# Seven-product sums seeded by a ScalarE copy in a second PSUM bank, and every engine's order given as a table

## The chip, the cores and the metric

The kernel runs on one core of a Trainium2 chip. The metric is the device time of one execution in microseconds, the median of several runs. The engines of the core are TensorE (PE in the profile; its weight loads are PEld), VectorE (DVE), ScalarE (ACT), GpSimd (POOL) and SyncE (SP). Here POOL issues the loads that cast from float32 to bfloat16, and some stores; SP issues transposing DMAs and the other stores.

## The reference

Sliding-window attention with a linear bias for 8 batches of 576 positions and 8 heads of 64, and then one mixer block on its output:

```
scores = q @ k.T / sqrt(64);  mask: 0 <= i - j < 128;  bias -slope[h] * |i - j|
x = softmax(scores) @ v                                  # (8, 576, 512)
h = relu(x.T @ w_tok1) @ w_tok2                          # 576 -> 256 -> 576, over positions
u = x + h.T
out = u + relu(u @ w_ch1) @ w_ch2                        # 512 -> 1536 -> 512, over channels
```

## The kernel before

The 576 positions of a batch are four blocks of 128 and a tail of 64; two batches share one tail block and make a pair (pairs 0 to 3). For each batch there is a *side* part (transposes of q and k, `scores`, exponentials, mask, `values`, then `token_mix`, which gives `u`) and a *main* part (the channel mixer). The side part of the next batch runs interleaved with the main part of this one. In the list of operations a plan's parts 2b+1 are main(b), and 2b are side(b).

The channel mixer's products are done as block products of a fast scheme with seven products instead of eight. `second` (L1246 and on) does so with `w_ch2`: each of the seven products is 128 x 256 outputs for two blocks, summed over six slices in two groups of six (`g` 0 and 1), L1326. They go to three banks: g2 takes products 1, 6, 7 and 4 one on top of the other, g1 product 2, g3 products 5 and 3. After product 1 a VectorE operation (`evict`, L1289) writes `ub` + g2 to an output tile `ob`; product 6 then adds onto g2, and when product 2 has ended in g1, a second `evict` adds g1 to that tile. The products stand in the order 1, 5, 6, 2, 3, 7, 4. `unit` (L976) does the same with `w_ch1` for some of the hidden slices (`UNITS`: nine units, in batches 3 to 7; the other slices go through `chunk`, L1085, as plain products): product 1 in bank y is copied to SBUF by `keep` (L1021, ScalarE), product 2 goes to bank z, and `join` adds the two on VectorE (L1030) and applies the ReLU (L1032). Product 6 adds onto y once the copy is made.

The banks: PSUM is eight banks of 128 x 512 float32. `plan.buf("ps", choice)` asks for one or for two side by side.

What sets the order. Nothing is issued as the code is read. Every step is an operation of a `Plan` with an engine, a cost, a rank and its dependences; `Plan.run` lets each engine take, greedily, the operation that is ready first (by the plan's costs), and among ready ones the lowest rank. Ranks are shifted by pseudo-random offsets (`SEEDS`, `SHIFT`). Some operations may go to ACT or to DVE, whichever would end first. The loads go on POOL's queue in the order of the list `LOADS` and then pair by pair; `qk` and `v` are rings of five blocks, so a load waits for the last user of the block that it overwrites. Where the plan sees PE idle in the first 60 us, `emit` puts products of zeros there (`spin`, L1418) that keep PE running.

The tail's way from token mix to channel mix: `token_mix` ends for the odd batch of a pair with products on half of the columns (L885), a VectorE sum writes `utl` (L907), a transposing DMA on SP makes `uTt` (L915), and `tail_piece` (L1129) multiplies it with `w_ch1`.

Of the kernel before, what the change touches and what calls it, by code (L numbers as in the profile page):

```python
# [10 lines left out]
ALU = mybir.AluOpType  # L11
# [8 lines left out]
class Buf:  # L20
    def __init__(self, ring, choice):
        self.ring, self.choice, self.slot = ring, choice, None
        self.writers, self.parts, self.users = [], {}, []
# [6 lines left out]
class Ring:  # L30
# [14 lines left out]
    def best(self, choice, skip=0):  # L45
        got = []
        for c in choice:
            ts = [self.free(i) for i in c]
            if None not in ts:
                got.append((max(ts), c))  # L50
        got.sort(key=lambda x: x[0])
        return got[skip] if len(got) > skip else None

    def take(self, b):
        b.slot = self.best(b.choice)[1]
        for i in b.slot:
            self.owner[i] = b
            self.log[i].append(b)
# [15 lines left out]
class Plan:  # L74
# [6 lines left out]
    def buf(self, name, choice=None):  # L81
        return Buf(self.rings[name], choice or self.rings[name].each)
# [46 lines left out]
    def run(self):  # L129
        ops = self.ops  # L130
        for o in ops:
            o.rank += SHIFT * offset(o)
# [82 lines left out]
        while todo:  # L215
            best = None
            for e, c in cand.items():
                pick, early = None, None
                for o in c:
                    if e == "POOL" and o is not pool[sent]:  # L220
                        continue
# [7 lines left out]
                    for b in o.bufs:  # L229
                        if b.slot is None:  # L230
                            got = b.ring.best(b.choice, asked.count(b.choice))
# [19 lines left out]
                if early and early[1] is not pick[1] and early[0][0] < pick[0][0] + GRACE * pick[1].cost:  # L251
# [13 lines left out]
            todo -= 1  # L265
            for b in o.bufs:
# [43 lines left out]
    def emit(self, spin):  # L310
        banks = self.rings["ps"]
        fills = []
        for a, z in self.gaps:
            if a < FILL and z - a > (250 if a > DENSE else 60):
                for i, log in enumerate(banks.log):
                    spans = [(min(u.t0 for u in b.users), max(u.done for u in b.users)) for b in log]
# [27 lines left out]
RELU = 350  # L344
SUMS_AT = 60e3
# [40 lines left out]
def kernel(  # L386
# [51 lines left out]
    def bank(choice=ONE):  # L438
        return plan.buf("ps", choice)
# [257 lines left out]
    def scores(pr, blk, half, rank, behind=()):  # L697
# [6 lines left out]
        sp = [bank(TWO + THIRD + [(6, 7)])] if joint else [bank(TWO + THIRD if first else TWO) for _ in range(2)]  # L704
# [13 lines left out]
        def go():  # L718
            for i in range(4):
                for kind, kb, a, z in work:  # L720
                    for e in range(2):
                        pe_.matmul(wide(e)[:, i, 0 if joint else kind, a:z],  # L722
                                   lhsT=ts[kb]()[e * D : (e + 1) * D, NHP + i, :],
                                   rhs=ts[blk]()[e * D : (e + 1) * D, i, a:z], start=not slanted, stop=True,
                                   skip_group_check=slanted)
# [105 lines left out]
    def token_mix(b, rank):  # L831
# [7 lines left out]
        t1 = [bank() for _ in range(NJ)]  # L839
# [20 lines left out]
        plan.op("PE", 225 if xt else 432, tails, rank(216), adds=t1,  # L860
# [11 lines left out]
        hts = []  # L872
        for blk in blocks:
            wide = b == 0
            if wide and blk < 2:
                hts.append(bank(TWO))
            ht = hts[blk % 2] if wide else bank()
# [3 lines left out]
            def go(blk=blk, ht=ht, hs=hs, fold=fold):  # L881
                for j in range(NJ):
# [4 lines left out]
                    else:  # L887
                        c = blk % NC
                        pe_.matmul(ht()[:, hs], lhsT=W2[:, j, c * P : (c + 1) * P], rhs=r1()[:, j, :],  # L889
                                   start=j == 0, stop=j == NJ - 1 and not fold)  # L890
# [5 lines left out]
            if blk == TAIL:  # L896
                rd += [(r1s[b - 1], j) for j in range(NJ)]
            tks = [(xb, (TAIL, 0)), (xb, (TAIL, 1))] if blk == TAIL and pr < HALVED else [(xb, (blk, None))]
            hop = plan.op("PE", 652 if fold else 436, go, rk, reads=rd + tks * fold, needs=lw2t if blk == TAIL else lw2,
                    mode=2 if blk == TAIL else 0, **({"adds": ht} if wide and blk > 1 else {"makes": ht}))  # L900
            if wide:
                wides.append(hop)
            if fold:
                plan.op("ACT", 600, lambda u=u_of(pr, blk)[1], ht=ht, hs=hs: act_.copy(out=u(), in_=ht()[:, hs]),
                        rk, part=u_of(pr, blk)[2], uses=[ht])
            else:
# [69 lines left out]
    def unit(b, u, rank, uT, tt, r2):  # L976

        y, z, w = [bank(ANY if b == B - 1 or BANKS == 8 else ONE) for _ in range(3)]
        e1, e2, e5 = [plan.buf("ob") for _ in range(3)]
# [56 lines left out]

        rk = product(1, y)
# [416 lines left out]
```

## Time and profile before

| | |
|---|---|
| three runs | 274.09, 274.43, 274.66 us; median 274.43 |
| profiled execution | span 273.4 us from its first to its last instruction, 1.0 less than the median of the runs |
| PE, PEld busy | 267.6 us (98%), 190.0 us (69%) |
| DVE, ACT, POOL busy | 230.4 us (84%), 148.9 us (54%), 112.9 us (41%) |
| granted TensorE clock | 0.999 |
| DMA | 38.71 MB, 142 GB/s in the mean |

In the rows of the profile a line stands with its engine, its operation and its tiles as out<-in. A busy PE includes the time in which a product waits in the array behind another, so its share says little by itself; the waits and the chain of work say more.

### The profile page before, as it was taken

How to read it: one execution, taken by the hardware profiler on the slowest of the kernel's cores; microseconds unless marked ns; L12 is line 12 of the kernel's file. 1: busy time of each engine (PE TensorE's matmuls, PEld its weight loads, DVE VectorE, ACT ScalarE, POOL GpSimd, SP SyncE). 2: the span in 40 equal slices, each digit the busy share in tenths (PEclk: the TensorE clock that was granted, in tenths of full speed). 3: DMA queues.
4: the chain of work that ended last, by engine and by line, in shares of the span. 5: the costliest groups of instructions: out<-in, count | busy, mean ns of one | idle time of the engine just before them, and what ended most of it. 6: DMA issues, size and time to landing. Idle time of an engine off the chain costs nothing.

```text
span 273.4 us, 7106 instructions
## 1 busy us (share of the span) xinstructions
PE 267.6 (98%) x2839; PEld 190.0 (69%) x2839; DVE 230.4 (84%) x543; ACT 148.9 (54%) x258; POOL 112.9 (41%) x142
## 2 busy tenths in 40 slices
PE   8999999999999999989999999999999999999994
PEld 4675667575568556765778868586578676888884
DVE  6577799998989499855999979998898899968984
ACT  5384895356931683038951079615960596047720
POOL 8999645950770077500890007800940300040000
PEclk9999999999999999999999999999999999999999
DMA  8999999999998999999999989999996800541016
GB/s 155 154 163 174 192 199 178 153 142 236 148 146 107 179 191 119 141 166 227 116 118 155 223 172 81 139 132 210 178 155 109 217 2 0 79 134 42 1 41 192
DMA packets 167553, 38.71 MB, mean 142 GB/s; under 512 B 155872, under 2 KB 166496, under 8 KB 167520
## 3 DMA queue, kind: packets, MB, share of 16 engines
q0 software_dynamic: 113936, 19.51, 91.7%
q1 hardware_dynamic: 51360, 18.10, 36.2%
q10 hardware_dynamic: 2224, 0.66, 1.2%
q8 instruction: 22, 0.36, 0.6%
q14 instruction: 11, 0.09, 0.1%
HBM read 35.85 MB, written 9.44 MB: 166 GB/s over the span
## 4 chain that ended last, share of the span: by engine, by line
PE 94%; DMA 3%; DVE 1%; issue 0%; DVEq 0%
PE ps L1326 25%; PE ps L1085 19%; PE ps L1006 10%; PE ps L802 7%; PE ps L722 7%; PE ps L847 5%; PE ps L889 4%; PE ps L1418 4%; PE ps L1129 4%; PE ps L1218 3%; DMA uTt<-utl 3%; PE ps L679 2%; PE ps L857 1%; PE ps L885 1%; PE ps L1070 1%; PE ps L924 1%
## 5 line engine op out<-in xcount | busy, mean ns | idle before, releaser
L535 POOL DMA_DIRECT2D v<-in_v_dram x40 | 34.5, 867 | 85.8 <-PE ps L802 84.0
L757 ACT ACTIVATE pe<-ps 128x1024 bf16<-128x1024 f32 (+1 forms) x62 | 56.0, 956 | 19.7 <-PE ps L722 19.5
L1085 PE MATMUL ps<-uT,WC 128*128 128x512 bf16 x232 | 55.4, 380 | 0.0
L1326 PEld LDWEIGHTS <-r 128*128 128x128 bf16 x372 | 35.8, 98 | 6.3 <-issue 0.8
L1091 ACT ACTIVATE r<-ps 128x512 bf16<-128x512 f32 x51 | 29.9, 599 | 18.4 <-PE ps L1085 18.1
L1085 PEld LDWEIGHTS <-WC 128*128 128x128 bf16 x232 | 21.1, 97 | 20.8
L535 POOL DMA_DIRECT2D qk<-in_q_dram x38 | 33.0, 878 | 2.8 <-DMA v<-in_v_dram 2.6
L535 POOL DMA_DIRECT2D qk<-in_k_dram x38 | 33.3, 890 | 1.4 <-DMA WC<-in_moe_w_ch_dram 1.0
L767 DVE TENSOR_TENSOR pe<-pe,mask 128x1024 bf16<-128x1024 bf16 (+1 forms) x50 | 32.4, 664 | 0.9 <-ACT pe L757 0.8
L1326 PEld LDWEIGHTS <-s 128*128 128x128 bf16 x288 | 27.6, 98 | 4.8 <-issue 0.5
L818 DVE TENSOR_TENSOR xb<-ps,rt 128x256 bf16<-128x256 f32 (+1 forms) x68 | 27.3, 416 | 0.7
L802 PEld LDWEIGHTS <-pe 128*128 128x128 bf16 (+1 forms) x560 | 22.4, 98 | 6.1 <-DVE pe L767 1.2
L802 PE MATMUL ps<-v,pe 128*128 128x65 bf16 (+1 forms) x560 | 26.1, 194 | 0.0
L1326 PE MATMUL ps<-WC,r 128*128 128x256 bf16 x192 | 24.4, 273 | 0.0
L1326 PE MATMUL ps<-WT,s 128*128 128x256 bf16 x192 | 23.9, 273 | 0.0
L1326 PE MATMUL ps<-WT,r 128*128 128x256 bf16 x180 | 22.1, 273 | 0.0
L722 PEld LDWEIGHTS <-qkT 64*128 64x128 bf16 x560 | 14.8, 94 | 10.5 <-issue 8.5
L744 ACT ACTIVATE pe<-ps 128x1024 bf16<-128x1024 f32 x7 | 7.2, 1022 | 26.1 <-PE ps L722 26.1
L907 DVE TENSOR_TENSOR ub<-ps,xb 128x512 bf16<-128x512 f32 x30 | 19.0, 683 | 0.8 <-PE ps L889 0.8
L722 PE MATMUL ps<-qkT 64*128 64x128 bf16 (+1 forms) x304 | 19.3, 216 | 0.1
L815 DVE RECIPROCAL rt<-ps 128x4 f32<-128x4 f32 (+1 forms) x76 | 12.6, 176 | 6.0 <-PE ps L802 5.1
L847 PE MATMUL ps<-xb,W 128*128 128x512 bf16 x64 | 16.4, 379 | 0.0
(118 smaller groups left out, 459.4 us busy)
## 6 DMA issues: line engine op xcount, KB each, us to landing
v<-in_v_dram POOLq DMA_DIRECT2D x32, 128.0 KB, 5.3
qk<-in_k_dram POOLq DMA_DIRECT2D x30, 128.0 KB, 5.4
qk<-in_q_dram POOLq DMA_DIRECT2D x30, 128.0 KB, 5.3
WC<-in_moe_w_ch_dram POOLq DMA_DIRECT2D x8, 384.0 KB, 10.0
out_dram<-raw SPq DMA_DIRECT2D x10, 256.0 KB, 2.5
out_dram<-raw SPq DMA_DIRECT2D x18, 128.0 KB, 3.1
out_dram<-ob SPq DMA_DIRECT2D x7, 256.0 KB, 2.5
out_dram<-raw POOLq DMA_DIRECT2D x5, 256.0 KB, 2.6
```

Source lines behind the costliest of these rows:

```text
L535: nc.gpsimd.dma_start(out=to()[p0 : p0 + n, :, :], in_=rows(src, b, s0, n))
L722: pe_.matmul(wide(e)[:, i, 0 if joint else kind, a:z], lhsT=ts[kb]()[e * D : (e + 1) * D, NHP + i, :], rhs=ts[blk]()[e * D : (e + 1) * D, ...
L757: act_.activation(out=pb()[:, e, :, lo:, c0:c1_], in_=wide(e)[:, :, lo:, c0:c1_], func=ACT.Exp, scale=scale)
L767: dve_.tensor_tensor(out=o, in0=o, in1=heads(mk, es), op=ALU.mult)
L802: pe_.matmul(view()[a:z, at, i, :], lhsT=pb()[:, e, i, kind, a:z], rhs=vb()[:, h, 0 : D + 1], start=m == 0, stop=m == len(mms) - 1, skip_g ...
L818: dve_.tensor_tensor(out=x4(), in0=view()[r0:r1_, :, :, 0:D], in1=rt()[r0:r1_, 0:n, :, :].broadcast_to([r1_ - r0, n, 4, D]), op=ALU.mult)
L847: pe_.matmul(t1[j]()[:, :], lhsT=W1[:, c, j * P : (j + 1) * P], rhs=xb()[:, blk, :], start=c == 0, stop=False)
L907: plan.op("DVE", 690, lambda blk=blk, u=u_of(pr, blk)[1], ht=ht, hs=hs: dve_.tensor_tensor(out=u(), in0=ht()[:, hs], in1=xb()[:, blk, :], ...
L1006: pe_.matmul(bk()[:, c * HS : (c + 1) * HS], lhsT=l(c, cb), rhs=r(cb), start=new and c == 0 and cb == 0, stop=cb == 1, skip_group_check=True)
L1085: pe_.matmul(ct()[:, :], lhsT=WC1[:, cb, t * P : (t + 1) * P], rhs=uT()[:, cb, :], start=cb == 0, stop=cb == NCB - 1)
L1091: plan.op("ACT", 600, lambda t=t, ct=ct: act_.activation(out=r2()[:, t, :], in_=ct()[:, :], func=ACT.Relu), rk, part=(r2, t), uses=[ct], o ...
L1326: pe_.matmul(of(bk, c), lhsT=l(t, c), rhs=w(t), start=first, stop=g == 1 and t == HK - 1, skip_group_check=True)
```

## The change

Three things change. First, where a later product's operand is the plain sum of two products, the first of the two is copied by ScalarE from its bank to a second bank, and the second product adds onto the copy there (a product that doesn't start a sum adds to what the bank holds). In `second` this takes the place of the `evict` after product 1 in batches 0 to 6: g2 is copied to g1, product 2 adds onto g1, and one `evict` brings both to the output tile. In `unit` it takes the place of the `keep` of product 1 and of a `join`: y is copied to z, product 2 adds onto z, and one ReLU (ScalarE, or VectorE where the table says so) reads z. A copy may also come ahead of the token mix's last products (`SEEDED`), but that list is empty.

Second, so that a product adds to the copy everywhere in the bank, the bank's last tenant must have been written by PE over its whole width. Such tenants are marked `full`; a bank for a copy (`seeded`) is only taken from one of them. The scores and the tail pieces start a sum once per bank, and not once per piece of it. No spin is put in a bank just ahead of a copy.

Third, `ORDER` lists for each engine its operations by number; `run` takes them in that order, and an operation that could go to ACT or DVE goes where the table has it. `SEEDS` has no effect on the order any more. POOL's loads are in the table too.

```diff
 class Ring:
-    def best(self, choice, skip=0):
+    def best(self, choice, skip=0, seeded=False):
         got = []
         for c in choice:
+            if seeded and not all(self.owner[i] is not None and self.owner[i].full for i in c):
+                continue
...
     def run(self):
         ops = self.ops
+        lists = {e: [ops[int(x)] for x in ORDER[e].split()] for e in ORDER}
+        for e, given in lists.items():
+            for o in given:
+                if o.eng != e:
+                    o.eng, o.cost, o.emit = o.other
+                o.other = None
+        at = dict.fromkeys(lists, 0)
...
-                    if e == "POOL" and o is not pool[sent]:
+                    if lists and o is not lists[e][at[e]] or not lists and e == "POOL" and o is not pool[sent]:
                         continue
...
+ORDER = {
+    "PE": """
+        162 161 159 157 192 179 163 194 166 169 168 170 176 173 181 186 189 205 199 207 212 202 215 224 221 218 225
...
+SEEDING = 600
+SEEDED = []
...
     def scores(pr, blk, half, rank, behind=()):
...
+                    new = not at and (not i if joint else i % 2 == 0) or not whole
                     for e in range(2):
                         pe_.matmul(wide(e)[:, i, 0 if joint else kind, a:z],
                                    lhsT=ts[kb]()[e * D : (e + 1) * D, NHP + i, :],
-                                   rhs=ts[blk]()[e * D : (e + 1) * D, i, a:z], start=not slanted, stop=True,
-                                   skip_group_check=slanted)
+                                   rhs=ts[blk]()[e * D : (e + 1) * D, i, a:z], start=new and not slanted, stop=True,
+                                   skip_group_check=True)
...
     def unit(b, u, rank, uT, tt, r2):
-        y, z, w = [bank(ANY if b == B - 1 or BANKS == 8 else ONE) for _ in range(3)]
-        e1, e2, e5 = [plan.buf("ob") for _ in range(3)]
+        y, z, w = [bank(ANY if b == B - 1 or BANKS == 8 else ONE, full=True, seeded=x == 1) for x in range(3)]
+        e2, e5 = [plan.buf("ob") for _ in range(2)]
...
         rk = product(1, y)
-        k1 = keep(e1, y, rk)
+        k1 = plan.op("ACT", SEEDING, lambda: act_.copy(out=z()[:, :], in_=y()[:, :]), rk, makes=z, uses=[y])
         rk = product(5, w)
         k5 = keep(e5, w, rk)
-        rk = product(2, z)
-        join(e1, z, up, lo, rk)
+        rk = product(2, z, [k1], False)
+        relu(z, up, lo, rk)
         rk = product(6, y, [k1], False)
...
     def second(b, rank, r2, ss, sums, ub):
-            evict(m, bk, *DONE[m])
+            if m == 1 and g1.seeded:
+                capt[1] = plan.op("ACT", SEEDING, lambda: act_.copy(out=g1()[:, :], in_=g2()[:, :]), rank(0) - EV,
+                                  makes=g1, uses=[g2])
+            else:
+                evict(m, bk, *DONE[m])
```

The next rows are in the order of the program, without times. First POOL's queue at the start, up to the first weights of the token mix (W_118 is W1, W1p its last 64 rows; qk and v are the blocks of the rings). Before, from the second load on:

```order
L535 DMA qk_68<-in_k_dram 64x8x64 x2
L535 DMA qk_67<-in_q_dram 128x8x64
L535 DMA qk_69<-in_k_dram 128x8x64
L535 DMA qk_69<-in_q_dram 128x8x64
L535 DMA v_72<-in_v_dram 128x8x64
L535 DMA v_73<-in_v_dram 128x8x64
L535 DMA v_74<-in_v_dram 128x8x64
L535 DMA v_75<-in_v_dram 64x8x64 x2
L535 DMA qk_68<-in_q_dram 64x8x64 x2
L535 DMA v_76<-in_v_dram 128x8x64
L535 DMA qk_70<-in_q_dram 128x8x64
L539 DMA W_118<-in_moe_w_tok_dram 128x4x256
```

and after, from the third on:

```order
L623 DMA v_72<-in_v_dram 64x8x64
L623 DMA qk_68<-in_k_dram 64x8x64
L623 DMA qk_69<-in_q_dram 128x8x64
L623 DMA qk_69<-in_k_dram 128x8x64
L623 DMA v_73<-in_v_dram 128x8x64
L623 DMA v_74<-in_v_dram 128x8x64
L623 DMA qk_68<-in_q_dram 64x8x64 x2
L623 DMA qk_68<-in_k_dram 64x8x64
L627 DMA W1p<-in_moe_w_tok_dram 64x256
L623 DMA v_75<-in_v_dram 128x8x64
L623 DMA v_76<-in_v_dram 128x8x64
L627 DMA W_118<-in_moe_w_tok_dram 128x4x256
```

Ahead of W1 stand, with the loads not shown (one whole block before, two after), nine whole blocks and six halves before, and eight wholes, five halves and W1p after.

Second, ScalarE in the main part of batch 5, where one unit and then the second products are done (pe is an exponential, r a ReLU, COPY to raw or ob the copy of a product to SBUF). Before:

```order
L1091 ACTIVATE r_103<-ps 128x512 x2
L757 ACTIVATE pe_87<-ps 128x1024 x2
L1091 ACTIVATE r_103<-ps 128x512 x2
L757 ACTIVATE pe_85<-ps 128x1024 x2
L824 ACTIVATE xb_92<-ps,rt_90 128x64 x4
L1021 COPY raw_107<-ps 128x512
L1021 COPY raw_108<-ps 128x512
L1021 COPY ob_110<-ps 128x512
L865 ACTIVATE r_98<-ps 128x512
L1034 ACTIVATE r_103<-r_103 128x2x256 x2
L1050 ACTIVATE r_103<-ps 128x2x256
```

and after:

```order
L848 ACTIVATE pe_85<-ps 128x1024 x2
L1194 ACTIVATE r_103<-ps 128x512
L1144 COPY ps<-ps 128x512
L848 ACTIVATE pe_86<-ps 128x1024
L1121 COPY ob_111<-ps 128x512
L1138 ACTIVATE r_103<-ps 128x2x256
L848 ACTIVATE pe_86<-ps 128x1024
L915 ACTIVATE xb_92<-ps,rt_91 128x64 x4
L1453 COPY ps<-ps 128x512
L956 ACTIVATE r_98<-ps 128x512
L1138 ACTIVATE r_103<-ps 128x2x256
```

The first of three copies to SBUF has become a copy from bank to bank (L1144), the unit lies between the exponentials now, and the copy of the second products (L1453) is new on this engine.

Third, SP's queue around the tail's transpose of pair 1 (the second pair, `uTt<-utl`). Before:

```order
L1303 DMA out_dram<-ob_110 128x256 x2
L668 DMA_TRANSPOSE qkT_80<-qk_67 128x8x128
L1306 DMA out_dram<-ob_111 128x2x256
L1306 DMA out_dram<-raw_108 128x2x256
L668 DMA_TRANSPOSE qkT_79<-qk_69 128x8x128
L915 DMA_TRANSPOSE uTt_102<-utl_95 128x4x128
L915 DMA_TRANSPOSE uT_101<-ub_94 128x4x128 x4
```

and after:

```order
L756 DMA_TRANSPOSE qkT_83<-qk_67 128x8x128
L756 DMA_TRANSPOSE qkT_80<-qk_71 128x8x128
L756 DMA_TRANSPOSE qkT_79<-qk_69 128x8x128
L1408 DMA out_dram<-ob_110 128x256 x2
L1408 DMA out_dram<-raw_109 128x256 x2
L1015 DMA_TRANSPOSE uTt_102<-utl_95 128x4x128
L1015 DMA_TRANSPOSE uT_101<-ub_94 128x4x128 x4
```

The transpose still stands ahead of the four of the batch; two stores of earlier batches are now what stands right ahead of it.

More of the change, by code (lines that the diff above doesn't have):

```diff
@@ L703, in scores @@
         joint = LOJOINT and lo and not slanted
-        sp = [bank(TWO + THIRD + [(6, 7)])] if joint else [bank(TWO + THIRD if first else TWO) for _ in range(2)]
+        whole = not slanted and c1_ - c0 == P
+        sp = ([bank(TWO + THIRD + [(6, 7)], full=whole)] if joint
+              else [bank(TWO + THIRD if first else TWO, full=whole) for _ in range(2)])
         pb = plan.buf("pe")
@@ L838, in token_mix @@
         r1 = plan.buf(f"r1{half}")
-        t1 = [bank() for _ in range(NJ)]
+        t1 = [bank(full=True) for _ in range(NJ)]
         tk = half if pr < HALVED else None
@@ L905, in token_mix @@
                         rk, part=u_of(pr, blk)[2], uses=[ht])
+            elif seed:
+                plan.op("ACT", 600, lambda u=u_of(pr, blk)[1], ht=ht: act_.copy(out=u(), in_=ht()[:, :]),
+                        rk, part=u_of(pr, blk)[2], uses=[ht],
+                        other=("DVE", 690, lambda u=u_of(pr, blk)[1], ht=ht: dve_.tensor_copy(out=u(), in_=ht()[:, :])))
             else:
@@ L1049, in unit @@
         rk = product(4, y, [j3], False)
-        mark(plan.op("ACT", 600, lambda: act_.activation(out=r2()[:, dn, lo], in_=half_of(y), func=ACT.Relu), rk,
-                     uses=[y], part=(r2, ("relu", dn.start, 0)),
-                     other=("DVE", 690, lambda: dve_.tensor_scalar(
-                         out=r2()[:, dn, lo], in0=half_of(y), scalar1=0.0, scalar2=None, op0=ALU.max))), dn)
+        relu(y, dn, lo, rk)
         return rk
@@ L1080, in chunk @@
         def chunk(t):
-            ct = first[t] if t < len(first) else bank()
+            ct = first[t] if t < len(first) else bank(full=True)
             def go(t=t, ct=ct):
```

74 lines of the change are left out of this document (52 added, 22 removed), and 54 rows, old and new, of the table ORDER.

## The prediction

> **What bounds it now.** I read the page first: its parts on busy time and on the chain that ended last.
>
> ```profile
> span 273.4 us, 7106 instructions
> PE 267.6 (98%) x2839; PEld 190.0 (69%) x2839; DVE 230.4 (84%) x543; ACT 148.9 (54%) x258; POOL 112.9 (41%) x142
> PE 94%; DMA 3%; DVE 1%; issue 0%; DVEq 0%
> ```
>
> TensorE is the chain nearly from end to end; VectorE, from which the change takes work, is 1% of it. So the next view is the waits, cut to PE: who held it up.
>
> ```profile
> PE ps L1418 <- DVE zero L499: 1.0, 1, 1.0
> PE ps L1129 <- DMA uTt<-utl: 0.9, 1, 0.9
> PE ps L924 <- DVE ub L907: 0.3, 1, 0.3
> ```
>
> Three waits, 2.2 us in all, one of them the first microsecond of the span. Not one is a wait for a copy, for a sum or for a bank in the seven-product parts. That doesn't mean that PE always did useful work: L1418 is `spin`, products of zeros that the planner puts where it expects PE to be idle. The windows and the chain, in order of time, show where:
>
> ```profile
> 0.00:20.00 20.00, 18.89 (x211) 12.11 (x212) 12.82 (x46) 11.71 (x19) 18.62 (x28) 1.00 1.80 158
> 140.00:160.00 20.00, 20.00 (x188) 16.36 (x186) 17.86 (x37) 4.26 (x7) 3.93 (x5) 1.00 1.52 180
> 220.00:240.00 20.00, 20.00 (x209) 15.18 (x205) 19.33 (x43) 10.77 (x20) 0.39 (x1) 1.00 0.20 29
> by line: PE ps L1418 33.0%; PE ps L679 11.8%; PE ps L722 10.0%; PE ps L802 8.6%; PE ps L1085 7.4%; PE ps L889 5.0%; PE ps L731 4.9%; PE ps L847 4.9%; PE ps L1070 2.4%; PE ps L924 1.8%; DVE ub L907 1.7%; PE ps L857 1.5%; DVE qkT L685 1.2%; P
> 1.00 3.27 PE ps L1418 x8
> 9.43 0.96 PE ps L1418 x5
> 20.57 0.84 PE ps L1418 x4
> 21.41 0.65 PE ps L847 x3
> ```
>
> The row "by line" is for the window 0 to 35 us: spins are 33.0% of it, 11.55 us, and they all lie before 30 us. From 40 us on PE has no hole that a view shows, but for the 0.9 us at L1129. In 220 to 240 us VectorE is at 19.33 of 20, so there it is close behind PE, but PE doesn't wait for it. What can be won is therefore in the start, in that one wait, and in the cost of PE's own changes between tilings; what can be lost is everywhere, since the order of every engine is new.
>
> **The parts, one by one.** Useful PE work stays the same. The two orders have 2839 and 2831 products; the eight that are gone are spins (51 before, 43 after).
>
> *Spins.* Counted in the two orders, the spins are 21,800 columns before and 18,624 after, 3,176 fewer. Priced by the mean of before, 11.55 us by 21,800 columns is 0.53 ns a column: −1.7 us. The two ends are the rows above: the first spin has 8 x 460 columns in 3.27 us (0.89 ns each, −2.8 us), the one at 9.43 has 5 of about 456 columns in 0.96 us (0.42 ns, −1.3 us). I take −1.7, the mean, since the spins that shrink are both early and late ones. This holds only if the waits under them really got shorter. What speaks for it is the order of the loads on POOL's queue, where each load is issued only after the one before:
>
> ```profile
> 1.37 2.42 POOL L535 DMA_DIRECT2D qk<-in_k_dram  x3 [0.30 <-issue]
> 5.65 0.89 POOL L535 DMA_DIRECT2D qk<-in_q_dram  x1
> 14.01 0.83 POOL L539 DMA_DIRECT2D W<-in_moe_w_tok_dram  x1
> 14.76 0.63 POOL L539 DMA_DIRECT2D W1p<-in_moe_w_tok_dram  x1
> 37.00 0.74 POOL L539 DMA_DIRECT2D WC<-in_moe_w_ch_dram  x1 [1.23 <-DMA WC<-in_moe_w_ch_dram]
> DMA to landing us min/median/max: 5.3/9.5/12.5
> 46.57 2.13 PE L1326 MATMUL ps<-WC,r 128*128 128x256 bf16 x18
> ```
>
> Ahead of W1 stood nine whole blocks and six halves; now it is eight wholes, five halves and the small W1p. A whole takes 0.89 us to issue, a half 0.77 (the x3 row is one whole and two halves), so 1.7 us less stand ahead, and W1p gives 0.6 of it back: W1 comes about 1.0 us earlier. PE's first use of W1 is the L847 row at 21.41, right behind a spin. The last piece of WC2, however, has the same loads ahead of it in both. It is issued at 37.00, and with the median of the weights' landings (9.5 us, the row of L539) it is there at 46.5; the second half of batch 0's first product needs it and is the second six of the eighteen from 46.57 on, at 47.2. That is a ceiling on what the start can win, and a rival below.
>
> A hole that no spin covers would cost more than its length. The first spin's 3,680 columns took 3.27 us, where 0.42 ns each gives 1.55: 1.7 us lost to a slow TensorE, while the clock in the window row already reads 1.00. The Trainium skill, "TensorE: Matmul & The Clock Gate", section "Part 1: The HAM clock gate", says that an idle window of about 3.4 us halves the clock until about as much busy time has passed; the start of this trace fits that, and its clock row doesn't show it. By that rule alone fewer spins are a risk: an estimate of 1.7 us for each uncovered hole of that length.
>
> *Changes of tiling on PE.* A row of sixteen score products (64 rows, run two at a time) and one of full products:
>
> ```profile
> 187.06 0.55 PE ps L722 x16
> 191.45 1.73 PE ps L1085 x8
> ```
>
> 1.73 by 8 is 0.216 us for 512 columns, so 0.054 for 128; sixteen in pairs are 0.43, and 0.12 remains for the change. In the two orders PE changes between whole, 64-row and half-wide tilings 99 and 94 times: 5 x 0.12 = −0.6 us; between 0 (if the changes that went were free) and −0.6.
>
> *Copies in place of sums.* In seven second products (all batches but the last) the sum after product 1 becomes a ScalarE copy from one bank to another; in nine units the copy to SBUF becomes a copy to a bank, and a sum and a ReLU become one ReLU.
>
> ```profile
> L1021 ACT COPY ob<-ps x8: 580/585/647, 137.1 to 252.3; 128x512 f32<-128x512 f32 x8
> L1289 DVE TENSOR_TENSOR raw<-ps,ub x20: 664/686/694, 51.2 to 264.7; 128x512 f32<-128x512 f32 x20
> L1030 DVE TENSOR_TENSOR r<-ps,raw x18: 661/684/692, 138.7 to 254.4; 128x512 bf16<-128x512 f32 x18
> L757 ACT ACTIVATE pe<-ps x62: 592/1018/1071, 7.9 to 223.9; 128x1024 bf16<-128x1024 f32 x52, 128x512 bf16<-128x512 f32 x10
> L1326 PE MATMUL ps<-WT,s 128*128 128x256 bf16 x192 | 23.9, 273 | 0.0
> ```
>
> VectorE loses 7 x 0.686 and 9 x 0.684, 11.0 us; part comes back, since the table gives it 11 more of the ReLUs of 512 columns and 7 of the tail's. None of it is on PE's path, so the term is 0, with 0.3 to win (the whole L924 wait). What could cost is the wait: product 2 and product 6 now both wait for the copy, and a copy that writes a bank is not in this trace. The nearest row is the copy to SBUF, 0.585. Shortest in the new order are three places (second products of batches 0, 2 and 4) where between the end of product 1 and product 6 lie 0.87 us of other PE work (four products of 512 columns, or their like). A product's end comes 0.165 us behind its slot (273 ns less 108 for 256 columns, half of 0.216), so the copy is done at 0.75: it holds by 0.1 us. From the other side: were ScalarE, which works in order, in the midst of an exponential of 1.02 us, the copy would be up to 0.9 us late, 16 copies 14 us. In the order the copies mostly stand behind exponentials whose scores ended 1.3 us or more earlier. I take 0.
>
> *The tail's transpose.* The one wait for a DMA, in order of time:
>
> ```profile
> 110.47 0.60 PE ps L885 x4
> 111.09 0.69 DVE utl L907
> 111.81 6.84 DMA uTt<-utl
> 118.69 1.03 PE ps L1129 x8
> 110.05 1.44 POOL L535 DMA_DIRECT2D qk<-in_q_dram  x2
> ```
>
> Before, 6.6 us of PE work stand between the product that makes `utl` (L885) and the first that uses it transposed (L1129); after, eleven groups of products with 5.5 us (six of 0.66, three of 0.43, two of 0.12). The transpose took 6.84 us because it was issued just behind a burst of loads (last row). With the same 6.84 us the wait would be 2.0 instead of 0.9 us, +1.1; in the new order the burst is released by values products that end about 4.6 us ahead of L885, not 4.3, and it is longer; if it has drained, −0.9. I take 0.
>
> **Sum.** −1.7 − 0.6 + 0 + 0 = −2.3, and 0.3 back for small late arrivals of a new order: −2.0. The profiled execution has a span of 273.4; the runs' median is 274.4, 1.0 more, and I keep that: 271.4 of span, **272.4 us**.
>
> **Rivals.**
> - *More is won.* The burst of loads has drained and the early spins were the ones that shrank: another 0.9 and 0.4, 271.1 us. Chance 0.15.
> - *The start is bound by the loads.* The second half of product 1 begins at 46.5 instead of 47.2, no earlier, and by the two orders 0.4 us more of other work stands ahead of it: 1.1 us won instead of 1.7; and the tail's wait grows by 0.5. Then −1.1 − 0.6 + 0.5 + 0.3 = −0.9, 273.5 us. For it speaks that POOL issues for 18.62 of the first 20 us. Chance 0.13.
> - *Slower: PE waits for the copies.* ScalarE's queue holds them behind exponentials and ReLUs that themselves wait for later products. From a mean of 0.125 us late over the 16 copies the gain of 2.0 is gone; with 0.2 us each, 3.2 us, it is 275.6. For it: three places hold by 0.1 us, and the bank copy has no row. Against it: no wait of PE for ACT in the trace, with copies just as close. Chance 0.22.
> - *A cold TensorE.* One hole in the start that the table doesn't foresee and no spin covers: the 1.7 us of the first spin lost once more, 274.1, no change. Chance 0.06.
> - *The change doesn't do what it says*, in that the copies would not spare VectorE: by the counts above it does, and VectorE isn't the bound. No chance of its own.
>
> The forecast has the remaining 0.44. 0.2% of the median, about what a measurement of this kernel can tell, is 0.55 us, so "the same" is 273.9 to 275.0. Faster: 0.44, 0.15 and most of the load-bound case, 0.69. Same: the cold case and the edge of two others, 0.08. Slower: 0.23. The range goes from 270.2 (both ends of the spins' price and the drained burst) to 275.6, the price of the late copies; it leaves some 0.05 below and 0.12 above.
>
> **What would show it.** Right: spins at about 9.8 us of the chain in the first 35 us instead of 11.55; L847 first at about 20 us; no wait of PE for ACT in the list of waits; the copies at about 0.59 us. Wrong: waits of PE for the ACT lines of the copies (L1144, L1453 of the new kernel), a wait at the tail's first product near 2 us, or holes after 40 us that stand in no term above.

## The result, and the profile after

The changed kernel runs in 278.06 us (median of four, 276.87 to 279.58), the kernel before, beside it on the same chip, in 274.26 (four, 273.83 to 274.66): a ratio of 1.014, interval 1.010 to 1.018. That is 3.8 us slower where 2.0 us faster was forecast, and outside the range.

First the page of the kernel after, its busy times and the engines of the chain that ended last:

```profile
span 276.3 us, 7051 instructions
PE 265.7 (96%) x2799; PEld 189.0 (68%) x2831; DVE 229.2 (83%) x542; ACT 145.4 (53%) x268; POOL 112.9 (41%) x142
PE 69%; DMA 12%; DVE 8%; issue 3%; ACT 3%; POOL 2%; SPq 1%; ACTq 0%; DVEq 0%
```

TensorE's share of the chain fell from 94% to 69%, and a quarter of the chain now runs through transfers, VectorE and ScalarE. (2831 products were loaded; 32 of their records are missing, so the busy time of PE says little. The loads are all there, and what follows goes by them.) Its list of waits, cut to PE, where before there were three:

```profile
PE ps L1232 <- DMA uTt<-utl: 1.1, 1, 1.1
PE ps L1528 <- DVE zero L587: 1.0, 1, 1.0
PE ps L767 <- DVE qk L638: 0.5, 2, 0.3
PE ps L813 <- DMA qkT<-qk: 0.5, 2, 0.3
PE ps L893 <- DVE r L1195: 0.4, 1, 0.4
PE ps L1188 <- DVE r L1195: 0.2, 1, 0.2
PE ps L813 <- DVE ob L1337: 0.2, 1, 0.2
PE ps L893 <- DVE pe L858: 0.2, 1, 0.2
```

The first two were there before (0.9 and 1.0). The rest is new and small: the casts of the raw blocks, head transposes, ReLUs, a sum, a mask. None is a wait for a copy. The copies themselves, from the groups:

```profile
L1144 ACT COPY ps<-ps 128x512 f32<-128x512 f32 x9 | 5.1, 582 | 13.0 <-PE ps L1106 12.9
L1453 ACT COPY ps<-ps 128x512 f32<-128x512 f32 x7 | 4.1, 580 | 7.5 <-PE ps L1432 7.4
```

They last 0.58 us (0.59 was expected), and between the end of each and the first product that needs it lie 0.05 to 2.28 us; ten of the sixteen have under 0.57.

To see where PE falls back, I weigh its products by their columns and ask when a given amount of useful work was done. What is left after that work is taken off is the time lost up to there (spins, waits, changes of tiling). The column "before, usual" is an execution of the same instructions in the same order (`buffer_before` below); the one whose profile the prediction shows has 1.2 us more from 104 us of work on, of which more later. Each column is one execution.

| useful work done, us | before, shown | before, usual | after | after with both mends and a buffer | redrawn from 17 us on |
|---|---|---|---|---|---|
| 16 | 15.27 | 15.10 | 14.69 | 14.87 | 15.14 |
| 24 | 16.11 | 15.93 | 15.97 | 16.16 | 16.04 |
| 32 | 16.26 | 16.08 | 16.63 | 16.81 | 16.34 |
| 96 | 19.84 | 19.66 | 20.10 | 20.36 | 19.48 |
| 104 | 21.23 | 20.08 | 21.70 | 20.87 | 19.69 |
| 144 | 22.49 | 21.35 | 23.73 | 22.76 | 21.16 |
| 224 | 24.80 | 23.65 | 26.74 | 25.06 | 23.65 |

After wins 0.4 to 0.6 us by 16, has lost it by 24 to 32 (40 to 49 us of the trace), and then loses, above all between 104 and 144 (125 to 168 us) and near 192. Against the usual execution of before it has also lost 1.2 us between 96 and 104, at the tail's transpose, where the shown one lost as much. The first loss is on VectorE. The window from 34.4 to 43.1 us of before, then of after, and pieces of after's chain in it:

```profile
34.40:43.10 8.70, 8.70 (x111) 5.20 (x109) 8.33 (x19) 7.76 (x15) 3.25 (x4) 1.00 1.50 195
```

```profile
34.40:43.10 8.70, 7.84 (x94) 4.74 (x94) 8.23 (x20) 7.17 (x10) 5.01 (x6) 1.00 1.41 198
```

```profile
34.43 0.18 DVE rt L906
...
36.46 1.29 DVE pe L858 x2
37.78 0.69 DVE r L1195
...
42.42 0.59 DVE r L1195
43.01 0.04 issue
43.06 1.02 PE ps L1188 x4
```

VectorE is as full as before (8.23 of 8.70), but now the chain stays on it from 34.4 to 43.1 us, and PE, which had no idle time there, is busy for 7.84. Twice a ReLU that frees a bank (37.78, 42.42) stands behind masks and normalisations.

The later loss has two roots. One is the order of SyncE. Of the 53 transposes, two landed less than 0.5 us ahead of their first product before; now seven do, five of them head transposes by 0.05 to 0.11 us. The worst of the loads that wait, and SyncE's queue ahead of it:

```profile
192.74 0.45 PEld L813 LDWEIGHTS <-qkT 64*128 64x128 bf16 x16 [0.78 <-DMA qkT<-qk]
185.08 5.43 SPq L756 DMA_TRANSPOSE qkT<-qk  x4
```

The transpose it waits for is the third of those four; its blocks had been in SBUF since 144.2 us, and the second, ahead of it, isn't needed before 195.6. (The load of head transposes at 189.13 us, which waits for no transfer, has 0.42 us of idle time ahead of it too, so about half of the 0.78 is the wait. PE's own row there books 0.3.)

The other is the buffers. Six hold a sum (or a kept product of a unit), a sum from the time VectorE begins it until its store has landed. This sum was complete at 91.5 us, and its store is issued at 217.8:

```profile
90.82 0.68 DVE L1394 TENSOR_TENSOR raw<-ps,ub 128x512 f32<-128x512 f32 x1
217.81 1.76 SPq L1408 DMA_DIRECT2D out_dram<-raw  x2
```

Over the 31 stores of whole sums that stand in SyncE's and GpSimd's lists, the time between the end of the sum and the issue of its store adds up to 550 us in after, 76 us in before (longest 7.7). With buffers parked like that, the others turn over so fast that VectorE meets a store that hasn't landed, and TensorE behind it waits for a bank (rows of VectorE and of PE):

```profile
158.00 0.69 DVE L1394 TENSOR_TENSOR ob<-ps,ub 128x512 f32<-128x512 f32 x1 [0.57 <-DMA out_dram<-ob]
159.41 0.21 PE L813 MATMUL ps<-qkT 64*128 64x128 bf16 x1 [0.18 <-DVE ob L1337]
```

Last, the end. Before, the tail's four stores were issued from 263.5 us on, and the last store landed 1.8 us after its issue. After, they are issued from 268.95 us on, three microseconds before PE's last product ends (before: six), and the last store takes 2.7 us:

```profile
268.95 2.40 SPq L1346 DMA_DIRECT2D out_dram<-raw  x4
271.44 1.09 SPq L1411 DMA_DIRECT2D out_dram<-ob  x2
272.63 0.44 SPq L1482 DMA_DIRECT2D out_dram<-raw  x1
```

### The profile page after: what moved, and what is told of

Read it like the earlier page. It is cut to its first block, busy times and chain, and to the rows that moved or that the text cites. A ratio compares the mean times of both kernels' runs of the same rounds, so it can differ in the third digit from the quotient of the medians.

```text
span 276.3 us, 7051 instructions
## 1 busy us (share of the span) xinstructions
PE 265.7 (96%) x2799; PEld 189.0 (68%) x2831; DVE 229.2 (83%) x542; ACT 145.4 (53%) x268; POOL 112.9 (41%) x142
## 4 chain that ended last, share of the span: by engine, by line
PE 69%; DMA 12%; DVE 8%; issue 3%; ACT 3%; POOL 2%; SPq 1%; ACTq 0%; DVEq 0%
PE ps L1432 18%; PE ps L1188 13%; PE ps L1106 9%; PE ps L813 6%; DMA qkT<-qk 5%; PE ps L893 5%; PE ps L938 4%; PE ps L981 4%; PE ps L1232 3%; PE ps L1322 2%; DMA raw<-in_k_dram 2%; DMA uTt<-utl 2%; DVE pe L858 2%; ACT pe L848 2%; DMA qk<-in_q_dram 1%
## 5 line engine op out<-in xcount | busy, mean ns | idle before, releaser
L848 ACT ACTIVATE pe<-ps 128x1024 bf16<-128x1024 f32 (+1 forms) x62 | 56.8, 958 | 40.5 <-PE ps L813 38.7
L1194 ACT ACTIVATE r<-ps 128x512 bf16<-128x512 f32 x40 | 22.9, 600 | 12.6 <-PE ps L1188 12.4
L893 PEld LDWEIGHTS <-pe 128*128 128x128 bf16 (+1 forms) x560 | 23.6, 98 | 7.3 <-DVE pe L858 1.4
L893 PE MATMUL ps<-v,pe 128*128 128x65 bf16 (+1 forms) x560 | 26.9, 194 | 0.9 <-DVE r L1195 0.4
L909 DVE TENSOR_TENSOR xb<-ps,rt 128x256 bf16<-128x256 f32 (+1 forms) x62 | 25.0, 415 | 0.8
L1432 PE MATMUL ps<-WC,r 128*128 128x256 bf16 x192 | 25.4, 273 | 0.0
L1432 PE MATMUL ps<-WT,s 128*128 128x256 bf16 x192 | 24.9, 273 | 0.0
L1007 DVE TENSOR_TENSOR ub<-ps,xb 128x512 bf16<-128x512 f32 x30 | 19.9, 682 | 1.9 <-PE ps L981 1.9
L1411 POOL DMA_DIRECT2D out_dram<-raw x5 | 3.6, 720 | 39.0 <-issue 27.8
L915 ACT ACTIVATE xb<-ps,rt 128x64 bf16<-128x64 f32 (+1 forms) x56 | 12.7, 338 | 7.2 <-DVE rt L906 7.2
```

What stands on the lines that cost most here:

```text
L848: act_.activation(out=pb()[:, e, :, lo:, c0:c1_], in_=wide(e)[:, :, lo:, c0:c1_], func=ACT.Exp, scale=scale)
L893: pe_.matmul(view()[a:z, at, i, :], lhsT=pb()[:, e, i, kind, a:z], rhs=vb()[:, h, 0 : D + 1], start=m == 0, stop=m == len(mms) - 1, skip_g ...
L909: dve_.tensor_tensor(out=x4(), in0=view()[r0:r1_, :, :, 0:D], in1=rt()[r0:r1_, 0:n, :, :].broadcast_to([r1_ - r0, n, 4, D]), op=ALU.mult)
L915: act_.activation(out=x4()[:, e, i, :], in_=view()[r0:r1_, e, i, 0:D], func=ACT.Copy, scale=rt()[r0:r1_, e, i, :])
L1007: plan.op("DVE", 690, lambda blk=blk, u=u_of(pr, blk)[1], ht=ht, hs=hs: dve_.tensor_tensor(out=u(), in0=ht()[:, hs], in1=xb()[:, blk, :], ...
L1194: plan.op("ACT", 600, lambda t=t, ct=ct: act_.activation(out=r2()[:, t, :], in_=ct()[:, :], func=ACT.Relu), rk, part=(r2, t), uses=[ct], o ...
```

## The experiments

All times are medians; "before" is the kernel before, beside them on the same chip (273.9 to 274.1 us). The numbers in the diffs are entries of the table, that is, operations.

**sp_mended.** Four entries of SyncE's list, pieces of it one to a line:

```diff
- 608 459 301 632 620
+ 608 632 459 301 620
- 868 948 869 870 595 463 867 964
+ 948 868 869 870 867 595 463 964
- 1092 1116 1104 1128
+ 1092 1104 1116 1128
```

> The changed kernel's table with four places of SyncE's list altered and nothing else: the head transpose issued at 90.89 us goes ahead of two stores, the one at 146.48 ahead of a u transpose, the u transpose at 151.51 ahead of two stores, and the one at 187.81 ahead of the one at 186.44. Three of them land 0.05 to 0.11 us before the first product that reads them in the changed kernel. Theory T (the table leaves no room, so TensorE waits for late transposes): the waits that the profile books at TensorE's loads for these tiles, 0.4 us near 151 us and 0.8 us near 192 us, shrink to the 0.3 of an ordinary switch of tiling, and the kernel ends 0.3 to 1.0 us earlier, about 277.4. Rival C (the time is lost to the copies in ScalarE): within 0.2 us of the changed kernel.

276.81 us, ratio 1.0109 (1.0092 to 1.0126). That is 1.25 less than the changed kernel, which ran on another chip; by the intervals of the two ratios a gain is likely, its size isn't settled. In its profile the wait near 192 us is gone, and the mend at 146 us cost something: two stores came later for it, and TensorE waited 0.7 us near 155 us for a sum that had no buffer.

**end_mended.** TensorE's, VectorE's and SyncE's lists:

```diff
- 1400 1413 1420 1416 1417 1414 1407 1427
+ 1400 1413 1407 1416 1417 1414 1420 1427
- 1360 1421 1418 1415 1384 1408 1401 1429
+ 1360 1401 1408 1418 1384 1415 1421 1429
- 1422 1409 1404 1430
+ 1404 1409 1422 1430
```

> The changed kernel's table with its last 15 us altered and nothing else: the last six products of the tail's second half trade places with a half product, so that the tail's last two sums and its four stores stand about 2 us earlier on VectorE and SyncE, and TensorE does as many products in as much time. Theory E (the tail's stores are still under way when the last stores are issued): the last store lands 1.8 us after its issue, as before the change, in place of 2.7, the span is 0.8 to 1.0 us shorter, and the 1.7 us outside the span may fall back to 1.0; 276.3 to 277.3. Rival: the landing is long for another reason; within 0.3 us of the changed kernel. If the sums now come late for the product that waits for them, TensorE loses 0.2 to 0.4 us there.

276.18, ratio 1.0083 (1.0066 to 1.0100). The tail's stores are issued at 266.26 instead of 268.95; the last store is issued at 272.45 (on ScalarE's queue, so it isn't among these rows of SyncE's), as late as in the changed kernel (272.63), and lands 1.75 us later, at 274.2 instead of 275.3:

```profile
266.26 2.41 SPq L1346 DMA_DIRECT2D out_dram<-raw  x4
269.09 0.40 SPq L1411 DMA_DIRECT2D out_dram<-raw  x1
270.01 1.72 SPq L1411 DMA_DIRECT2D out_dram<-ob  x2
271.83 0.41 SPq L1482 DMA_DIRECT2D out_dram<-raw  x1
```

So theory E holds, for 1.1 us of landing in these two profiles. PE's last product ends no earlier (271.9 against 272.0 us), since this execution has a wait of its own in the middle, for a u transpose in an order that wasn't touched there:

```profile
PE ps L1188 <- DMA uT<-ub: 1.1, 1, 1.1
```

The time outside the span did not fall: it is 1.7 to 1.8 us in every timed execution of both kernels.

**sp_end_mended.** Both.

> Both mends of the table together. If they do not touch each other the gains add: theories T and E 275.8 to 276.9, still above the kernel before; rival C: no change.

275.82, ratio 1.0068 (1.0055 to 1.0081): clearly better than the change, and still 1.9 us behind before. Its profile has a new largest wait, the one that the later stores brought:

```profile
155.25 0.42 DVE L1337 TENSOR_TENSOR ob<-ps,utl 128x256 f32<-128x256 f32 x1 [1.32 <-DMA out_dram<-ob]
155.73 0.81 PE L1322 MATMUL ps<-WT,r 128*128 128x256 bf16 x6 [0.97 <-DVE ob L1337]
```

**sums_in_table.** The old sums in the new order; the two edits in the unit, `seeded` taken from the bank of the second product (its sum then stands in VectorE's list), and every PSUM tile pinned to the bank that it has in the changed kernel. The kept product of a unit takes one of the six buffers again, as before the change:

```diff
-        k1 = plan.op("ACT", SEEDING, lambda: act_.copy(out=z()[:, :], in_=y()[:, :]), rk, makes=z, uses=[y])
+        k1 = keep(e1, y, rk)
...
-        rk = product(2, z, [k1], False)
-        relu(z, up, lo, rk)
+        rk = product(2, z)
+        join(e1, z, up, lo, rk)
```

> The old sums put back in the new order: the first products of the seven-product sums are kept and added by VectorE and ScalarE as before the change, each new addition standing on VectorE where the copy stood on ScalarE (or just ahead of the relu), everything else in the table's order and in the same PSUM banks. Rival C (the copies cost the time): faster than the changed kernel, 274 to 277. Theory T (the copies are covered, the order is what loses): slower than the changed kernel, since the additions queue behind other work of VectorE in an order that was drawn without them; 16 places with 0.05 to 2.3 us of room behind the copy, so 2 to 8 us, 280 to 286.

287.22, ratio 1.0483 (1.0469 to 1.0497): 9 us slower than the change, a little more than expected. VectorE works 238.3 us instead of 229.2, and PE now waits for what it and ScalarE keep and join:

```profile
PE ps L1137 <- ACT ob L1152: 2.0, 1, 2.0
...
PE ps L924 <- DVE r L1161: 1.3, 2, 0.9
```

Rival C, that the copies cost the time, falls. In this order they spare it; that says nothing yet on whether they gain in another.

**copies_twice.** Each copy done twice, in both places:

```diff
-lambda: act_.copy(out=z()[:, :], in_=y()[:, :])
+lambda: [act_.copy(out=z()[:, :], in_=y()[:, :]) for _ in range(2)]
```

> The changed kernel with each of its 16 copies into the second bank done twice, so that it is through about 0.57 us later; nothing else differs. The room between the end of a copy and the first product that adds up on it or overwrites what it read is 0.05 to 2.3 us in the changed kernel's profile; 10 of the 16 have under 0.57, and what they lack adds up to 2.3 us. Theory T (TensorE does not wait for the copies as they are, and the cover is thin): 1.5 to 2.5 us slower than the changed kernel, 279.5 to 280.6. Rival C (TensorE waits for copies already): 16 times 0.57, 9 us slower. If the cover is wide: no change.

281.57, ratio 1.0270 (1.0254 to 1.0286), 3.5 us slower than the change. The two rows of waits for the copies add up to 2.1 us, what the room lacked (2.3):

```profile
PE ps L1106 <- ACT ps L1144: 1.2, 3, 0.5
...
PE ps L1432 <- ACT ps L1453: 0.9, 3, 0.3
```

Another 1.4 us came behind them (0.8 of it booked to a u transpose that landed late). So the copies are covered as they are, and the cover is thin, as theory T had it; what a delay sets off further on was left out of the expectation.

**copies_by_the_rules.** `ORDER = {}`: the copies without the table.

> The copies alone: the table is left out, and the planner's rules draw the order as before the change, with the numbers that shift ranks as they were. Theory T: those numbers were fitted to the old sums, and a product that is copied must now stand ahead of the one that adds up on it; slower than both kernels, 280 to 300. Rival (the copies gain by themselves and the table spoils it): 271 to 274.

296.12 (two executions), ratio 1.0798 (1.0778 to 1.0818), inside what theory T expected. The copies need an order drawn for them; the rules' numbers, as they are, give a bad one.

**redrawn_with_room.** 204 of TensorE's 514 places, 305 of VectorE's 509, 96 of GpSimd's 137, 61 of SyncE's 82 and 53 of ScalarE's 201 differ from the changed kernel's table.

> The change whole, with its copies; the table is drawn once more, by moving single entries of the five lists and keeping what shortens the plan when every transpose and load is taken to land 0.4 us (or transposes 0.7 us) later, every operation of VectorE and ScalarE to last 12 ns longer and every wait to be answered 20 ns later than the kernel's planner assumes. The end is as in the mended kernel. Theory T (the table loses because nothing in it may come late): the waits that the mended kernel still shows on TensorE behind 30 us (1.0 us for a sum that stood behind a store, 0.4 and 0.3 for relus, 0.3 to 0.5 for head transposes) go, and 2 to 3.5 us with them: 272.3 to 273.8, no slower than the kernel before. Rival (the copies and the new reach of the PSUM banks cost something that no order gives back): 275 or more.

278.07, ratio 1.0129 (1.0108 to 1.0149). That is 4 us above the range of theory T, and as a time it is what the rival foresaw; the profile shows another reason than the rival's. The late transposes are gone from its waits. In their place VectorE's timeline has a copy that waits for a store, and PE's list of waits a product that waits for what VectorE does behind that copy:

```profile
166.17 0.69 DVE L1122 COPY raw<-ps 128x512 f32<-128x512 f32 x1 [2.33 <-DMA out_dram<-raw]
```

```profile
PE ps L1106 <- DVE xb L909: 2.2, 1, 2.2
```

Stores had not been among the things taken to be late. This miss led to the buffers.

**one_more_buffer.** Both mends, and

```diff
-    plan.ring("ob", raws + [sb.tile([P, DM], F32, name=f"ob{i}") for i in range(2)])
+    plan.ring("ob", raws + [sb.tile([P, DM], F32, name=f"ob{i}") for i in range(3)])
```

> The table with both mends, and a seventh buffer for the sums that are stored, in place of six. In the mended kernel VectorE waits 1.3 us at 155 us for a store to land before it may write into its buffer, and TensorE waits 1.0 us behind it. Theory T (small waits of this kind are the rest of the loss): 0.5 to 1.0 us faster than the mended kernel, 274.8 to 275.3. Rival: the buffer was not the limit, within 0.2.

274.49, ratio 1.0020 (1.0009 to 1.0032): 1.3 us better than the same without it, and 0.4 us slower than before. VectorE's wait for a store is 0.6 us in its profile instead of 1.3, and PE's wait behind it 0.2 instead of 1.0.

**one_store_earlier.** One entry:

```diff
- 301 632 620 789
+ 301 632 451 620 789
- 1251 1263 451 1317
+ 1251 1263 1317
```

> One entry of SyncE's list moved and nothing else: the store of a sum that VectorE finishes at 91.5 us, and that the changed kernel issues at 217.8 us, is issued at about 92. Theory S (six buffers hold the sums until they are stored; the table leaves one full for 126 us, so the others turn over too fast for their stores to land): VectorE's wait for a store near 158 us (0.57 us) goes, with the bank that TensorE waits for behind it; 0.5 to 2 us faster than the changed kernel, 276.1 to 277.6. Rival (the late transposes and the end are the loss, the buffer is idle anyway): within 0.2 us.

276.65, ratio 1.0095 (1.0081 to 1.0110), 1.4 us less than the change (on another chip; 1.2 by the ratios), in the range of theory S. VectorE has no wait for a store left. But the waits that theory S named were 0.57 us on VectorE and 0.2 on PE, less than the gain. In this profile the tail's transpose also lands early (4.1 us after its issue, 5.8 in the changed kernel's), and PE's wait of 1.1 us for it is gone. How much of the gain the store brought isn't settled by this run alone. **buffer_alone**, the seventh buffer with the table as it is, asks the same question from the other side:

> The changed kernel with a seventh buffer for stored sums and its table as it is. Theory S: worth about what the one store is worth, 0.5 to 2 us, 276.1 to 277.6. Rival: within 0.2 us of the changed kernel.

276.29, ratio 1.0104 (1.0072 to 1.0136; two of the six executions were near 278 to 279), in the range, and with the same early landing of the tail's transpose in its profile. The cleaner answer is the pair above, with both mends and without or with the buffer: there the transpose landed early in both profiles. And **buffer_before**, the kernel before with its order written out and a seventh buffer:

> The kernel before, its order written out as a table (the same instructions in the same order on each engine), with a seventh buffer. Its VectorE shows no wait for a store and its stores are issued 0 to 8 us after their sums. Theory S: within 0.3 us of the kernel before. Rival (a seventh buffer helps either kernel): 0.5 to 1.3 us faster, and then the gain above is no answer to the question.

274.05, ratio 1.0000 (0.9990 to 1.0010). The buffer isn't a gain that either kernel could have had: it makes good what the table parks.

**one_store_and_mends.** The one store, the mended end, and the mends of SyncE's list without that at 146 us.

> The same store moved, with the mended end and three of the four mends of SyncE's list (without the one at 146 us, which put two stores off behind a transpose). Theory S with T and E: as good as the mended kernel with a seventh buffer, which ran in 274.5; 274.2 to 275.2. Rival: as the mended kernel without a buffer, 275.8.

275.97, ratio 1.0066 (1.0043 to 1.0090): what the rival foresaw, no better than without the store. Three of its six executions took 274.7 to 275.4, three 276.5 to 276.7; the profiled one is of the second kind and has the wait for the tail's transpose, 1.2 us, as much as lies between the two; the first kind has no profile. Whether the store adds to the mends isn't settled by it.

**redrawn_behind_40** and **redrawn_from_17.** Both with the seventh buffer and the mended end; 183 and 228 of TensorE's places, 280 and 324 of VectorE's, 45 and 51 of SyncE's, 84 and 102 of GpSimd's moved.

> The copies, the mended end and the seventh buffer; single entries of the table that stand between 40 and 250 us are moved, and what shortens the plan is kept, with transposes 0.4 to 0.7 us later, loads up to 0.4 us later, stores 1 to 2 us later, VectorE's and ScalarE's operations 6 to 12 ns longer and waits 10 to 20 ns longer than the planner assumes. The redrawn kernel before this one left the stores out of that list and lost 2.2 us behind one. Theory T (the order is all of the loss): of the waits that the kernel with seven buffers books on TensorE behind 40 us (0.3 to 0.5 us at two transposes, 0.2 to 0.4 us at two sums, a relu and a mask) most go, 0.8 to 1.5 us: 273.0 to 273.7, as fast as before or a little faster. Rival (what is left is the price of the copies): 274.3 to 275.

> As the kernel beside it, with the entries from 17 us on moved too. In the changed kernel the chain runs on VectorE from 34.4 to 43.1 us, and the 0.6 us won by 35 us are lost there. Theory T: another 0.3 to 0.7 us, 272.4 to 273.4, faster than the kernel before. Rival: no different from the kernel beside it, and the start's gain can't be kept.

274.45 (ratio 1.0017, 1.0008 to 1.0026) and 274.39 (1.0023, 1.0009 to 1.0037; executions from 273.63 to 275.87). Both miss the expectation for theory T, as a time, and both fall where the rivals stood (274.3 to 275; no different from the kernel beside it). In its profiled execution (273.99 us, one of its faster ones) the second does have PE free of waits, all of them gone but for the start:

```profile
PE ps L1528 <- DVE zero L587: 1.0, 1, 1.0
PE ps L981 <- DMA W<-in_moe_w_tok_dram: 0.4, 1, 0.4
PE ps L767 <- DVE qk L638: 0.3, 1, 0.3
```

and the table above shows what that is worth: at 224 us of work it has lost 23.65 us, to the hundredth what the kernel before loses in its usual execution. So in this execution neither the copies nor the new rule for the banks cost PE anything. What makes the median 0.4 us longer than that execution, and whether it is a price of the copies, stays open. No version beats the kernel before.

## Why the prediction was wrong

*The reading of the bound* was right, and it should have decided more. TensorE was the chain, and work taken from VectorE brought nothing. Of the 11 us little was left in any case: VectorE's busy time fell from 230.4 to 229.2 us, since the table gives it ReLUs that ScalarE did before. With all waits gone, in the one execution that shows it, the copies' kernel is as fast as before and no faster.

*Spins, −1.7: the premise failed.* The columns did shrink, the spins' busy time fell from 13.9 to 11.8 us, and L938's first weights are loaded at 20.5 us where L847 started at 21.4; 0.4 to 0.6 us was won by 31 us. But a spin is only where the planner expects a hole. The holes that replaced them are plain waits (for the casts at L638, for two ReLUs), and by 40 us nothing was left. The step called VectorE 1% of the chain and priced moves on it at nothing; from 34.4 to 43.1 us it is the chain.

*Changes of tiling, −0.6:* not seen. The order without waits, with about as many changes as the table has, loses as much as before. No run measures this alone.

*Copies, 0:* right, in size (0.58 us) and in that PE doesn't wait for them. The margin was put at 0.1 us in three places; these measured about 0.25, and the tightest of the sixteen, 0.05, is another.

*The tail's transpose, 0:* 1.1 for 0.9 us, right against the profile that was read, and by luck, for that execution was an exception. With less work as cover (the 5.5 us for 6.6 of the prediction) a landing after 6.84 us was to cost 2.0; it took 5.8. In the usual execution of the kernel before (`buffer_before`) the transpose lands after 4.3 us and PE doesn't wait for it at all. Against that the changed kernel's profiled execution loses 1.2 us here. No profile of a single mend has that late landing (3.9 to 4.3 us), so up to 1.1 us of each mend's gain may be this and not the mend.

*"0.3 back for small late arrivals of a new order": this is the term that failed most.* It stood in the sum without a row under it. On PE the new late arrivals cost 2.5 us against the profile shown (from −0.6 at 16 us of work to +1.9 at 224), and the end, which was given no term, another 0.8 between PE's last product and the end of the span. Together that is 3.3 us for the 0.3, and the 1.7 of the spins didn't come. Mending the order and its buffers brings the kernel from 3.8 to 0.4 us behind before (274.49), without touching a copy. How it divides is less sure: the end 1.1 us by its landings, the seventh buffer 1.3 beside the mends, one parked store up to 1.4, four transposes up to 1.2, the single ones each measured against a kernel whose executions differ by 2.7 us, and not simply additive.

*"1.0 outside the span":* it is 1.75. The execution whose profile the prediction shows has a span of 273.4; those timed beside the experiments have 271.9 to 273.0. It is one in which the tail's transpose lands late, so a wait was read that the kernel seldom has. The forecast's time isn't touched by it, since the 1.0 was taken off and put back.

*The rivals.* The slower one had the right sign by the wrong mechanism and with too small a size (275.6): what came late were transfers, stores and VectorE's ReLUs, not the copies. The load-bound start, as it was put, isn't borne out: PE has no wait for weights, and from 34.4 us on the chain is VectorE's. The chain of after does begin with the first load of k (6.75 us from 1.27 on), where that of before ran through spins. Of the signs of being wrong that the prediction gave, the last is the one that came: holes after 40 us that stand in no term.

## What to carry to other kernels

When one engine is the whole chain, price an edit by the holes it closes on that engine and by nothing else, and treat a new order as a risk in itself: for each transfer count the time from landing to first use, and for each buffer the time from ready to stored, in the old order and the new. Both counts can be had from the two orders and the plan's times before anything runs (here a store moved behind 120 us of other work), and both told against this change. An order that is drawn by trying against a plan can use up what the plan doesn't charge for (the redrawn order that took stores to be on time lost 2.2 us behind one), so leave it room in the latencies that the trace shows to vary. And look at more than one execution: a wait in the one profile may be the exception.

## What the runs showed of the hardware

- The tail's transpose of pair 1, issued at 111 to 114 us behind a burst of loads, varies from one execution to the next. In two profiles of the kernel before's order it landed 4.3 and 6.8 us after its issue; in ten of the changed table and its mends, eight times after 3.8 to 4.4 us and twice after 5.8 and 6.0. The later landing came with 0.9 to 1.2 us of wait on PE. In the three redrawn orders it took 3.2, 4.5 and 5.3 us.
- The last store of the kernel, 128 KB, landed 1.75 us after its issue where four others had been issued in the four microseconds ahead (`end_mended`), and 2.7 us after it where there were seven (after). The groups of stores in after have medians of 2.4 to 4.1 us. A buffer stays taken until then: VectorE's wait at 158 us ends with a landing. The Trainium skill, "DMA: Bandwidth & Descriptors", section "Anatomy of one DMA — SWDGE (gpsimd) path", puts the fixed cost of a transfer that GpSimd issues at about 2 us, most of it the wait for the write to be confirmed. GpSimd's stores in before agree, with medians of 2.5 and 2.6 us for 256 KB, movement included; the 1.75 us are of a store that ScalarE issues, of which that section doesn't speak.
- A copy of 128x512 from bank to bank takes ScalarE 570 ns (its median; 580 on the mean), from bank to SBUF 585. The Trainium skill, "ScalarE: Activation LUTs", section "Step-by-step: what each stage is for", says that ScalarE writes PSUM faster than SBUF. The runs agree, by 15 ns, too little to choose by.
